# One rounding from VectorE to ScalarE, a score product moved between value products, and an earlier turn of the row of maxima in an attention and soft-MoE kernel

## The chip, the cores and the metric

The kernel runs on one core of one Trainium2 chip. The metric is the device time of one execution in microseconds, lower is better. Engines are named as in the profile: PE is TensorE (PEld its weight loads), DVE is VectorE, ACT is ScalarE, POOL is GpSimd, and SP is the engine that issues the DMAs.

## The reference

Eight batches of eight heads of causal attention with a decay, 576 positions and 64 channels a head, and behind it a soft mixture of eight experts. Cut to what matters here:

```python
scores = scale * np.matmul(q, k.transpose(0, 1, 3, 2))
decay = cum[:, :, :, None] - cum[:, :, None, :]
scores = np.where(causal, -1000000000.0, scores + decay)
scores = scores - np.max(scores, axis=-1, keepdims=True)
attn = np.exp(scores)
attn = attn / (np.sum(attn, axis=-1, keepdims=True) + 1e-09)
attn_out = np.matmul(attn, v)
logits = x @ phi
```

`x` is the attention output as 4608 tokens of 512 channels. The logits then feed a softmax over the tokens (dispatch) and one over the slots (combine), the experts' two products, and the output.

## The kernel before, in words

The 64 heads are taken as 32 pairs. The order of all instructions is written out by hand: each engine runs its own queue in the order in which the code emits it, and waits on semaphores where it needs another engine. An opening does pair 0, parts of pair 1 and the first scores of pair 2; then a loop (line 725 on, `for g in range(1, NG)`) runs one slot for each pair; then a tail does the experts and the output. Scores are computed twice.

First, `s1` (L230, PE) makes scores of queries in rows, with rounded operands, into a PSUM bank named `s`, and `tops` (L244, L246, DVE) takes the maximum of each row of it into a column of `MT`. A head has six such products, numbered 0 to 5. A slot g does the second head of pair g+1 (called u0) and the first head of pair g+2 (u1). When both heads of pair g+1 have their maxima, `mturn` (L256, PE) transposes the columns of `MT` into a PSUM bank, `mrows` copies them out on ACT (L265) and sends them by a DMA from SP (L268, `YA<-mr`) into a row of the operand `YA`. The maxima are thereby subtracted inside the second product.

Second, `s2` (L283 and L284, PE) makes the scores of head h0 and h1 of pair g, keys in rows, into one of three `ring` banks, as a rounded product (L283: `YA`, `WA`) and a correction by the low parts (L284: `YB`, `WB`); `expo` (L290, ACT) takes the exponential of a bank into `PTS`. Segments 0, 1, 2 have a bank each, and segments 3 to 5 share one. `causal` (L298, L301, POOL) blanks the upper triangle. `s3` (L315, PE) multiplies by the values into `pv`, 100 instructions a slot. `norm` (L330 to L335, DVE) divides into `X`. `px` (L342, PE) transposes `X`, and `xcopy` (L372 to L377, ACT) copies it out to `XTS` for the logits.

Operands are prepared ahead: `round_k` (L183) and `round_q` (L188) round on ACT, `dup_q` (L203) and `dup_k` (L199) send the rounded halves by DMA to other partitions, `low_k` and `low_q` (L209, L214, POOL) subtract, and `load_cum` (L194) loads two rows of cumulated decay into `WA`. All DMAs of the loop are issued by SP in one queue.

With `b, w = divmod(g - 4, 4)`, the slots with w = 2 (g = 6, 10, ..., 30) have in addition `combine(b, 0)`, two DVE instructions (L495, L496) ahead of the slot's `tops`, and `dispatch` (L475, PE) ahead of the values. Slots with w = 1 have `mtop` and others.

In the opening the places of the change are the DVE copy of line 625, which rounds the queries of the second head of pair 1; `round_k(1, 1)` (line 630), `expo(0, 3)` (line 631), `dup_q(1, 1, 2)` and `load_cum(2)` behind it; `mturn(1, 0, 1)`, which turns the maxima of head 2; and the stretch from line 654 to 668 with `first(4, 0)`, the first two score products of the first head of pair 2, beside the values of pair 0. `SIDES[0]` is a list of twenty products. `warm(1, cs)` puts PE work without a result into the next `ring` bank.

In the loop they are the two ACT copies of `xcopy(g - 1, (4,))` (L372), `mturn(g + 1)` and `expo(h1, 2)`.

Of the kernel before, what the change touches and what calls it, by code (L numbers as in the profile page):

```python
# [20 lines left out]
NG = B * NPAIR  # L21
# [49 lines left out]
SIDES = [[x for n in zip(units(h, 0, range(4)), units(h, 1, range(4))) for x in n] for h in range(2)]  # L71
# [4 lines left out]
def attn_softmoe(ctx: ExitStack, tc: tile.TileContext, qk, v, f, phi, w1, w2, cst, out):  # L76
    nc = tc.nc
# [102 lines left out]
    def round_k(g, *hs):  # L180
        if pair(g):
            for h in hs or range(2):
                nc.scalar.copy(WA[g % 3][0:64, S * h : S * h + S], RAW[g % 3][64:128, h])  # L183

    def round_q(g, *hs):
        if pair(g):
            for h in hs or range(2):
                nc.scalar.copy(YA[g % 3][0:64, h, 64:640], RAW[g % 3][0:64, h])  # L188
# [45 lines left out]
    def tops(i, *which):  # L234
        if not head(i):
            return
        g, h = divmod(i, 2)
        for n in which:
            bank, o, blk, j0, w = TOPS[n]
            t = st["top", i % 2, bank]  # L240
            m0 = max(448 - (128 * blk + 64) + j0, 0)
            top = MT[g % 3][:, NBLK * h + blk : NBLK * h + blk + 1] if g else m2[h][:, blk, 1:2]
            if n == 2:
                nc.vector.tensor_reduce(top, t[:, o : o + w], axis=AX.X, op=ALU.max)  # L244
                continue
            nc.vector.tensor_tensor_reduce(  # L246
                out=t[:, o : o + w], in0=t[:, o : o + w], in1=mask[:, m0 : m0 + w], scale=1.0, scalar=top.bitcast(F32) if n == 3 else -3.0e38,
                op0=ALU.add, op1=ALU.max, accum_out=top,
            )

    def mturn(g, h0=0, h1=2):

        if not pair(g):
            return
        pm = pv[h0 and 1][:, 384:512]
        nc.tensor.transpose(pm[0 : NBLK * (h1 - h0), 0:128].bitcast(F32R), MT[g % 3][:, NBLK * h0 : NBLK * h1], turner)  # L256
        st["pm", g, h0] = pm
# [29 lines left out]
    def expo(i, bank):  # L287
        if head(i):
            t, at = st["bank"]
            nc.scalar.activation(PT[i % 2][:, SEG_O[bank] : SEG_O[bank] + at], t[:, 0:at], AF.Exp, scale=0.125)  # L290
# [20 lines left out]
    def s3(g, todo):  # L311
        for h, t, u, c in todo:
            r = queries(t, u)
            at = pt_col(c, 64 * r)
            nc.tensor.matmul(  # L315
                pvv[h][64 * u : 64 * u + 64, t, :], PT[h][:, at : at + 64], V[:, g % 2, c, 65 * h : 65 * h + 65], start=(c == 0), stop=(c == r // 2)
            )
# [47 lines left out]
    def xcopy(g, ts):  # L365
        if pair(g):
            n, o = TURN[ts[0]]
            to = XT[g % NPAIR]
            if ts == (4,):
                for h in range(2):  # L370
                    r = slice(64 * h, 64 * h + 64)
                    nc.scalar.copy(to[r, 128:192], pv[n][r, o + 64 * h : o + 64 * h + 64])  # L372
            elif ts == (0, 3):
                to = to[:, 0:384].rearrange("p (n c) -> p n c", c=192)[:, :, 0:128]
                nc.scalar.copy(to, pv[n][:, o : o + 256].rearrange("p (n c) -> p n c", c=128))
            else:
                nc.scalar.copy(to[:, PLACE[ts[0]] : PLACE[ts[0]] + 128 * len(ts)], pv[n][:, o : o + 128 * len(ts)])  # L377
# [221 lines left out]
    def first(i, n, busy=0):  # L599
        s1(i, *GROUPS[n])  # L600
        warm(busy, cs)
        tops(i, *GROUPS[n])

    def both(i, n):
        s2(i, *((0,), (1,), (2,), (3, 4, 5))[n])
        expo(i, n)
# [15 lines left out]
    both(0, 1)  # L622
    first(2, 0)
    both(0, 2)
    nc.vector.tensor_copy(YA[1][0:64, 1, 64:640], RAW[1][0:64, 1])
    next(r1)
    first(2, 1)
    next(r1)
    s2(0, 3, 4, 5)
    round_k(1, 1)  # L630
    expo(0, 3)
    dup_q(1, 1, 2)
    dup_k(1, 1, 2)
# [18 lines left out]
    first(3, 2)  # L652
    first(3, 3)
    round_k(2, 0)
    both(1, 3)
    causal(1)
    low_k(3)
    low_q(3)
    round_q(2, 0)
    s3(0, SIDES[0])  # L660
    mturn(1, 1, 2)
    mrows(1, 1, 2)
    first(4, 0)
    round_k(2, 1)
    round_q(2, 1)
    dup_q(2)
    dup_k(2)
    s3(0, LAST[0])
    norm(0)
    first(4, 1)  # L670
    s3(0, LAST[1] + SIDES[1][:8])
# [53 lines left out]
    for g in range(1, NG):  # L725
        h0, h1 = 2 * g, 2 * g + 1
        u0, u1 = h0 + 3, h0 + 4
        b, w = divmod(g - 4, NPAIR)
        c = b - 1 if w == 0 else b if (b, w) == (B - 2, 3) else None
        if g < 4:  # L730
            load_v(g + 1)
            load_qk(g + 3)
        else:
            load_qk(g + 3)
            load_v(g + 1)
        if 2 <= g < NRES + 2:
            wload(g - 2)
        if w == 1:
            weigh(b)
        low_q(h0 + 2)  # L740
        low_q(h1 + 2)
        s2(h0, 0)
        expo(h0, 0)
        norm(h0 - 1)
        if w == 1:
            mgroup(b)
        if w == 2:
            combine(b, 0)
        s1(u0, 2)
        tops(u0, 2)  # L750
        s2(h0, 1)
        expo(h0, 1)
        s1(u0, 3)
        tops(u0, 3)
        if 1 < g < NG - 1:
            px(g - 1, 0)
        s2(h0, 2)
        expo(h0, 2)
        if g == NG - 1:
            px(g - 1, 0)  # L760
        if g > 1:
            px(g - 1, 3)
        else:
            round_k(3, 0)
            round_q(3, 0)
        s1(u0, 0, 1)
        tops(u0, 0, 1)
        if g > 1:
            px(g - 1, 1)
        s2(h0, 3)  # L770
        if g > 1:
            xcopy(g - 1, (0, 3))
            px(g - 1, 2)
            xcopy(g - 1, (1, 2))
        s2(h0, 4)
        s1(u0, 4, 5)
        s2(h0, 5)
        expo(h0, 3)
        tops(u0, 4, 5)
        causal(h0)  # L780
        low_k(h0 + 2)
        if w == 1:
            mtop(b)
        s2(h1, 0)
        expo(h1, 0)
        if g == 1:
            for t in (0, 3, 1, 2):
                px(0, t)
        px(g - 1, 4)
        if g == 1:  # L790
            xcopy(0, (0, 3))
            xcopy(0, (1, 2))
        xcopy(g - 1, (4,))
        s1(u1, 2)
        tops(u1, 2)
        s2(h1, 1)
        expo(h1, 1)
        s1(u1, 3)
        tops(u1, 3)
        s2(h1, 2)  # L800
        if g < NG - 2:
            expo(h1, 2)
        mturn(g + 1)
        mrows(g + 1)
        if g >= NG - 2:
            expo(h1, 2)
        s1(u1, 0, 1)
        tops(u1, 0, 1)
        s2(h1, 3, 4)
        s1(u1, 4, 5)  # L810
        s2(h1, 5)
        expo(h1, 3)
        tops(u1, 4, 5)
        causal(h1)
        low_k(h1 + 2)
        if g == 1:
            round_k(3, 1)
            round_q(3, 1)
        load_cum(g + 3)
        dup_q(g + 2)  # L820
        dup_k(g + 2)
        if g == 29:
            sides[2].close()
            p2 = fresh(ctx, "p2", 2)
            wstream(*p2, RAW[30 % 3])
        if g == 30:
            sides[1].close()
            xp = ctx.enter_context(tc.tile_pool(name="xp", bufs=1))
            X.append(xp.tile([P, NBLK, 256], F32, name="X3"))
            p0 = fresh(ctx, "p0", 1)  # L830
            p1 = fresh(late, "p1", 3)
            wstream(*p0, *p1, RAW[31 % 3])
        if g == 31:
            sides[0].close()
            with tc.using_default_side("right"):
                tp = ctx.enter_context(tc.tile_pool(name="tp", bufs=1))
            cT = tp.tile([P, sum(CUT)], F32R, name="cT")
            wstream(tp.tile([P, QW], F32, name="w36"))
        if w == 1:
            mcast(b)  # L840
        if c is not None:
            combine(c, 1)
        if w == 2 and b < B - 2:
            dispatch(b, *range(NBLK))
        if g == NG - 1:
            st["lg", B - 1] = scratch(False, f"lg{B - 1}")
            nc.vector.memset(st["lg", B - 1][:, 128:192], -1.0e30)
        round_k(g + 3)
        if w == 1:
            weigh2(b)  # L850
            total(b)
        round_q(g + 3)
        if c is not None:
            combine(c, 2)
        s3(g, VALUES[:30])
        norm(h0)
        if g == 31:
            logits(B - 1, 0, 1)
            wstream(XTS[:, 0:QW], PTS[:, 0:QW])
            split(0, 0)  # L860
            split(1, 0)
        s3(g, VALUES[30:])
        if w == 0:
            logits(b, *range(NPAIR))
        if w == 1:
            tokens(b, 0, 1)
        if g == 28:
            wstream(RAW[29 % 3])
# [272 lines left out]
```

## Time and profile before

| | us |
|---|---|
| runs of the kernel before | 390.41, 391.46, 395.79 |
| their median | 391.46 |
| the profiled execution, its own time | 392.3 |
| its span, first to last instruction | 390.6 |

The span is what the views show; 1.7 us of the profiled execution lie around it. The profiled execution is 0.84 us above the median. Busy shares of the span are PE 95%, PEld 85%, DVE 72%, ACT 69%, POOL 65%. Matmuls overlap and their ends are modelled, so a busy PE can hide a gap shorter than about a matmul's length; the starts of successive instructions tell more.

### The profile page before, as it was taken

To read this page: it belongs to the slowest core of one execution; us is meant where nothing else is said; L and a number is where in the kernel's file an instruction comes from. 1 tells how busy PE (TensorE), PEld (TensorE's weight loads), DVE (VectorE), ACT (ScalarE), POOL (GpSimd) and SP (SyncE) were. 2 spreads that over 40 slices of the span, in tenths; PEclk is the share of its full clock that TensorE was granted. 3 is DMA by queue.
4 is the path that set the end of the run, shared out by engine and by line. 5 is a ranking of instruction groups with operands and counts; after the bars stand their busy time and mean duration, and the time that the engine had idled before them with its cause. 6 is when DMAs were issued, how large, how long until landed. Compare 5 with 4: busy or idle time off the path is not lost.

```text
span 390.6 us, 15123 instructions
## 1 busy us (share of the span) xinstructions
PE 370.5 (95%) x5863; PEld 330.7 (85%) x5863; DVE 281.7 (72%) x1080; ACT 271.3 (69%) x669; POOL 255.0 (65%) x357
## 2 busy tenths in 40 slices
PE   7999999999999999999999999999999998999870
PEld 7789999999999999999999999999999885567640
DVE  7978887878887788788878887878787534341681
ACT  8869887878787778787878787878786553021560
POOL 4897887878787878787878787878787821000000
PEclk9999999999999999999999999999999998999995
DMA  6875978777777777777777777777775899995798
GB/s 205 205 195 148 283 223 278 189 233 207 224 211 215 213 212 214 213 214 211 213 214 214 211 214 212 214 214 212 212 227 154 269 350 377 407 417 206 264 393 314
DMA packets 34344, 93.72 MB, mean 240 GB/s; under 512 B 4266, under 2 KB 8288, under 8 KB 34272
## 3 DMA queue, kind: packets, MB, share of 16 engines
q1 hardware_dynamic: 34272, 92.75, 76.4%
q8 instruction: 46, 0.75, 0.8%
q14 instruction: 26, 0.21, 0.2%
HBM read 63.93 MB, written 9.73 MB: 189 GB/s over the span
## 4 chain that ended last, share of the span: by engine, by line
PE 86%; DMA 6%; POOL 2%; DVE 1%; ACT 1%; issue 1%; POOLq 0%; DVEq 0%; ACTq 0%
PE pv L315 24%; PE ring L283 14%; PE s L230 13%; PE ring L284 13%; PE pv L342 5%; PE pv L981 4%; PE more L941 4%; PE lg L389 3%; DMA out<-RAW 3%; PE ds L475 2%; DMA YA<-mr 2%; DMA WB<-WA 1%; POOL WB L209 1%; DMA PTS<-in_f 1%; POOL YB L214 1%
## 5 line engine op out<-in xcount | busy, mean ns | idle before, releaser
L290 ACT ACTIVATE PTS<-ring 128x320 f32<-128x320 f32 (+2 forms) x256 | 118.1, 502 | 49.3 <-PE ring L284 36.4
L283 PE MATMUL ring<-YA,WA 67*128 67x320 f32 (+9 forms) x384 | 121.5, 330 | 0.8 <-DMA YA<-mr 0.8
L246 DVE CUSTOM_DVE_ANT_0 s<-s,mask 128x320 f32<-128x320 f32 (+3 forms) x256 | 109.0, 442 | 5.6 <-PE s L230 1.1
L284 PE MATMUL ring<-YB,WB 128*128 128x320 f32 (+4 forms) x384 | 110.4, 296 | 0.0
L315 PE MATMUL pv<-V,PTS 128*64 128x65 f32 x3200 | 101.9, 223 | 0.2 <-POOL WB L209 0.2
L315 PEld LDWEIGHTS pv<-V,PTS 128*64 128x64 f32 x3200 | 96.9, 138 | 3.1 <-issue 1.5
L230 PE MATMUL s<-WA,YA 66*128 66x288 f32 (+9 forms) x384 | 98.2, 310 | 0.8 <-DMA RAW<-in_qk 0.4
L209 POOL TENSOR_TENSOR WB<-RAW,WB 64x576 fp32r<-64x576 f32 x64 | 90.4, 1412 | 11.1 <-DMA WB<-WA 5.8
L214 POOL TENSOR_TENSOR YB<-RAW,YA 64x576 fp32r<-64x576 f32 x64 | 89.7, 1421 | 2.6 <-POOL EX L397 0.2
L283 PEld LDWEIGHTS ring<-YA,WA 67*128 67x128 f32 (+3 forms) x384 | 69.7, 183 | 6.3 <-issue 2.1
L284 PEld LDWEIGHTS ring<-YB,WB 128*128 128x128 f32 (+1 forms) x384 | 70.0, 182 | 0.1
L230 PEld LDWEIGHTS s<-WA,YA 66*128 66x128 f32 (+1 forms) x384 | 62.9, 190 | 7.4 <-ACT PTS L290 1.5
L301 POOL TENSOR_SCALAR_AFFINE_SELECT PTS<-PTS 128x128 f32<-128x128 f32 (+1 forms) x128 | 31.5, 268 | 21.1 <-ACT PTS L290 18.6
L246 DVE DVE_READ_ACCUMULATOR2_ANT MT<- 128x1 fp32r x310 | 43.8, 141 | 0.0
L298 POOL TENSOR_SCALAR_AFFINE_SELECT PTS<-PTS 128x384 f32<-128x384 f32 x64 | 33.5, 523 | 14.2 <-ACT PTS L290 10.3
L342 PE MATMUL pv<-cs,X 128*128 128x128 f32 x155 | 42.0, 277 | 0.0
L183 ACT CAST WA<-RAW 64x576 fp32r<-64x576 f32 x64 | 40.1, 668 | 1.0 <-DMA RAW<-in_qk 0.2
L188 ACT CAST YA<-RAW 64x576 fp32r<-64x576 f32 x63 | 39.6, 671 | 0.4
L246 DVE CUSTOM_DVE_ANT_0 s<-s,mask,MT 128x288 f32<-128x288 f32 x62 | 32.6, 526 | 9.3 <-PE s L230 0.4
L330 DVE TENSOR_SCALAR rl<-pv 128x5 f32<-128x5 f32 x64 | 10.5, 164 | 34.0 <-PE pv L315 23.6
L335 DVE TENSOR_TENSOR X<-pv,rl 128x320 f32<-128x320 f32 (+1 forms) x65 | 31.5, 486 | 2.4 <-DMA YA<-mr 0.3
L244 DVE TENSOR_REDUCE MT<-s 128x1 fp32r<-128x288 f32 x62 | 27.8, 449 | 0.4 <-PE s L230 0.4
(221 smaller groups left out, 389.2 us busy)
## 6 DMA issues: line engine op xcount, KB each, us to landing
w<-in_w SPq DMA_DIRECT2D x45, 512.0 KB
RAW<-in_qk SPq DMA_DIRECT2D x31, 576.0 KB
V<-in_v SPq DMA_DIRECT2D x32, 325.0 KB
YB<-YA SPq DMA_DIRECT2D x30, 288.0 KB
WB<-WA SPq DMA_DIRECT2D x30, 288.0 KB
p<-in_w SPq DMA_DIRECT2D x6, 512.0 KB
out<-RAW SPq DMA_DIRECT2D x6, 512.0 KB
out<-p SPq DMA_DIRECT2D x5, 512.0 KB
```

The lines of the kernel that those rows point to most:

```text
L183: nc.scalar.copy(WA[g % 3][0:64, S * h : S * h + S], RAW[g % 3][64:128, h])
L188: nc.scalar.copy(YA[g % 3][0:64, h, 64:640], RAW[g % 3][0:64, h])
L209: nc.gpsimd.tensor_tensor(t[0:64], RAW[g % 3][64:128, h], t[64:128].bitcast(F32), op=ALU.subtract)
L214: nc.gpsimd.tensor_tensor(YB[g % 2][64:128, h], RAW[g % 3][0:64, h], YA[g % 3][0:64, h, 64:640].bitcast(F32), op=ALU.subtract)
L230: nc.tensor.matmul(t[:, o : o + w], ya[0:m, h, 128 * blk : 128 * blk + 128], wa[0:m, j0 : j0 + w], start=True, stop=True)
L246: nc.vector.tensor_tensor_reduce(out=t[:, o : o + w], in0=t[:, o : o + w], in1=mask[:, m0 : m0 + w], scale=1.0, scalar=top.bitcast(F32) if ...
L283: nc.tensor.matmul(o, wa[0:m, j0 : j0 + n], ya[0:m, h, 64 + i0 : 64 + i0 + w], start=True, stop=False)
L284: nc.tensor.matmul(o, wb[:, j0 : j0 + n], yb[:, h, i0 : i0 + w], start=False, stop=True)
L290: nc.scalar.activation(PT[i % 2][:, SEG_O[bank] : SEG_O[bank] + at], t[:, 0:at], AF.Exp, scale=0.125)
L298: nc.gpsimd.affine_select(d3, d3, pattern=[[0, 3], [1, 128]], compare_op=ALU.is_ge, fill=0.0, base=0, channel_multiplier=-1)
L315: nc.tensor.matmul(pvv[h][64 * u : 64 * u + 64, t, :], PT[h][:, at : at + 64], V[:, g % 2, c, 65 * h : 65 * h + 65], start=(c == 0), stop= ...
L342: nc.tensor.transpose(pm[:, 0:128], x[:, t, 128 * (p % 2) : 128 * (p % 2) + 128], ident)
```

## The change

In the opening the rounding of line 625 goes from DVE to ACT, behind `round_k(1, 1)`. `round_q(2, 0)` goes ahead of `both(1, 3)`, and so ahead of its exponential. `first(4, 0)` goes ahead of `mturn(1, 1, 2)`; the list of values is cut at 20, which is the whole of `SIDES[0]`, so the twenty products stay together. In the slots from g = 2 on, `mturn` and `mrows` go ahead of `s2(h1, 2)`, and `xcopy(g - 1, (4,))` goes behind them. `expo(h1, 2)` comes behind them on ACT; before, that was so in the last slots only.

```diff
@@ -622,12 +622,12 @@
     both(0, 1)
     first(2, 0)
     both(0, 2)
-    nc.vector.tensor_copy(YA[1][0:64, 1, 64:640], RAW[1][0:64, 1])
     next(r1)
     first(2, 1)
     next(r1)
     s2(0, 3, 4, 5)
     round_k(1, 1)
+    round_q(1, 1)
     expo(0, 3)
     dup_q(1, 1, 2)
     dup_k(1, 1, 2)
@@ -652,20 +652,20 @@
     first(3, 2)
     first(3, 3)
     round_k(2, 0)
+    round_q(2, 0)
     both(1, 3)
     causal(1)
     low_k(3)
     low_q(3)
-    round_q(2, 0)
-    s3(0, SIDES[0])
+    s3(0, SIDES[0][:20])
+    first(4, 0)
     mturn(1, 1, 2)
     mrows(1, 1, 2)
-    first(4, 0)
     round_k(2, 1)
     round_q(2, 1)
     dup_q(2)
     dup_k(2)
-    s3(0, LAST[0])
+    s3(0, SIDES[0][20:] + LAST[0])
     norm(0)
     first(4, 1)
     s3(0, LAST[1] + SIDES[1][:8])
@@ -790,20 +790,23 @@
         if g == 1:
             xcopy(0, (0, 3))
             xcopy(0, (1, 2))
-        xcopy(g - 1, (4,))
+        if g == 1:
+            xcopy(0, (4,))
         s1(u1, 2)
         tops(u1, 2)
         s2(h1, 1)
         expo(h1, 1)
         s1(u1, 3)
         tops(u1, 3)
+        if g > 1:
+            mturn(g + 1)
+            mrows(g + 1)
+            xcopy(g - 1, (4,))
         s2(h1, 2)
-        if g < NG - 2:
-            expo(h1, 2)
-        mturn(g + 1)
-        mrows(g + 1)
-        if g >= NG - 2:
-            expo(h1, 2)
+        expo(h1, 2)
+        if g == 1:
+            mturn(g + 1)
+            mrows(g + 1)
         s1(u1, 0, 1)
         tops(u1, 0, 1)
         s2(h1, 3, 4)
```

On PE in the opening, in the difference of the two orders, the twenty value products of pair 0 (one row, x20), the first score products of pair 2 (`s_0`) and the turn of the maxima of pair 1 (`MT_110`):

```order
 L284 MATMUL ring_153<-YB_91,WB_92 64x64
 L315 MATMUL pv_149<-V,PTS 64x65 x20
+L230 MATMUL s_0_395<-WA_94,YA_93 128x320
+L230 MATMUL s_0_395<-WA_94,YA_93 128x192
 L256 MATMUL pv_150<-turner,MT_110 5x128
-L230 MATMUL s_0_399<-WA_94,YA_93 128x320
-L230 MATMUL s_0_399<-WA_94,YA_93 128x192
 L315 MATMUL pv_149<-V,PTS 64x65 x5
```

The two score products and the turn have changed places; the values ahead of them are where they were.

On PE in the second half of slot 4 (its other slots from 2 to 30 read alike), the first-pass products of u1 (`s_2`, `s_0`), the turn of the maxima of pair 5 (`MT_111`) and the two instructions of `s2(h1, 2)` (`ring_151`):

```order
 L283 MATMUL ring_153<-YA_85,WA_86 128x320
 L284 MATMUL ring_153<-YB_91,WB_92 128x320
-L230 MATMUL s_2_985<-WA_90,YA_89 128x288
+L230 MATMUL s_2_983<-WA_90,YA_89 128x288
+L256 MATMUL pv_149<-turner,MT_111 10x128
 L283 MATMUL ring_151<-YA_85,WA_86 128x320
 L284 MATMUL ring_151<-YB_91,WB_92 128x320
-L256 MATMUL pv_149<-turner,MT_111 10x128
 L230 MATMUL s_0_995<-WA_90,YA_89 128x320
```

The turn stands two instructions earlier, straight behind the product `s_2`.

On ACT in the second half of slot 5 (a slot like the others), the exponentials of h1 (128x448, then two of 128x320, then 128x512), the copies of `xcopy` and the copy of the row of maxima (`mr`):

```order
 L290 ACTIVATE PTS<-ring_153 128x512
 L290 ACTIVATE PTS<-ring_151 128x448
-L372 COPY XTS<-pv_150 64x64 x2
-L290 ACTIVATE PTS<-ring_152 128x320
-L290 ACTIVATE PTS<-ring_153 128x320
-L265 CAST mr_0_1171<-pv_149 10x128
+L290 ACTIVATE PTS<-ring_152 128x320
+L265 CAST mr_0_1166<-pv_149 10x128
+L372 COPY XTS<-pv_150 64x64 x2
+L290 ACTIVATE PTS<-ring_153 128x320
 L290 ACTIVATE PTS<-ring_151 128x512
```

The copy of the row stood behind two copies and two exponentials; it now stands behind one exponential, and the copies and the second exponential follow it.

## Rows read from the trace of the kernel before

**Rows 1.** The page, part 1: busy time and share of the span, PE.
```profile
PE 370.5 (95%) x5863; PEld 330.7 (85%) x5863; DVE 281.7 (72%) x1080; ACT 271.3 (69%) x669; POOL 255.0 (65%) x357
```

**Rows 2.** Waits of PE from 8 to 310 us: us in total, times, longest.
```profile
PE ring L283 <- DMA YA<-mr: 0.5, 1, 0.5
PE s L230 <- DMA RAW<-in_qk: 0.4, 1, 0.4
PE pv L256 <- POOL WB L209: 0.3, 1, 0.3
PE pv L315 <- POOL WB L209: 0.2, 1, 0.2
```

**Rows 3.** Timeline of the opening, 16.0 to 19.2 us: start, us, engine, line, instruction.
```profile
15.43 1.32 DVE L625 CAST YA<-RAW 64x576 fp32r<-64x576 f32 x1
...
16.09 0.67 ACT L183 CAST WA<-RAW 64x576 fp32r<-64x576 f32 x1
...
16.78 0.47 SPq L203 DMA_DIRECT2D YB<-YA  x1
...
17.57 0.40 PE L230 MATMUL s<-WA,YA 66*128 66x320 f32 x2
...
17.93 0.45 SPq L194 DMA_DIRECT2D WA<-cumd  x1
...
18.13 0.49 PE L511 MATMUL ring<-cs 128*128 128x192 f32 x2
...
18.61 0.14 DVE L246 DVE_READ_ACCUMULATOR2_ANT MT<- 128x1 fp32r x1
...
18.89 0.22 PE L256 MATMUL pv<-turner,MT 128*5 128x128 f32 x1 [0.28 <-POOL WB L209]
```

**Rows 4.** Timeline of the opening, 20.7 to 22.7 us.
```profile
20.75 1.39 PE L315 MATMUL pv<-V,PTS 128*64 128x65 f32 x40
...
22.20 0.50 PE L230 MATMUL s<-WA,YA 66*128 66x320 f32 x2
```

**Rows 5.** Windows of 1 us: length, engines (none here), PEclk, DMA share, GB/s.
```profile
20.00:21.00 1.00, 1.00 0.26 64
```

**Rows 6.** Timeline of slot 4, an ordinary slot, 48.15 to 48.9 us.
```profile
48.20 0.14 DVE L246 DVE_READ_ACCUMULATOR2_ANT MT<- 128x1 fp32r x1
...
48.43 0.31 PE L283 MATMUL ring<-YA,WA 98*128 98x320 f32 x1
...
48.44 0.42 ACT L372 COPY XTS<-pv 64x64 f32<-64x64 f32 x2
48.57 0.31 PE L284 MATMUL ring<-YB,WB 128*128 128x320 f32 x1
...
48.72 0.22 PE L256 MATMUL pv<-turner,MT 128*10 128x128 f32 x1
```

**Rows 7.** Timeline of the same slot, 48.8 to 50.0 us, ACT.
```profile
48.88 0.77 ACT L290 ACTIVATE PTS<-ring 128x320 f32<-128x320 f32 x2
...
49.53 0.24 ACT L265 CAST mr<-pv 10x128 fp32r<-10x128 f32 x1
```

**Rows 8.** Timeline of slot 10, a slot with `combine`, 114.9 to 115.8 us.
```profile
115.08 0.31 PE L283 MATMUL ring<-YA,WA 67*128 67x320 f32 x1
...
115.17 0.14 DVE L246 DVE_READ_ACCUMULATOR2_ANT MT<- 128x1 fp32r x1
...
115.36 0.08 PEld L256 LDWEIGHTS pv<-turner,MT 128*10 128x10 f32 x1
...
115.39 0.30 PEld L230 LDWEIGHTS s<-WA,YA 97*128 97x128 f32 x2
```

**Rows 9.** Line 495, the first instruction of `combine`: ns min/median/max, first and last start.
```profile
L495 DVE TENSOR_REDUCE sm<-tk x7: 326/326/327, 73.2 to 304.2; 128x5 f32<-128x160 f32 x7
```

**Rows 10.** The chain that ended last, 110 to 131 us: start, us, what.
```profile
126.45 3.80 DMA YA<-mr
```

**Rows 11.** Timeline of PE behind slot 30, 303 to 314 us.
```profile
312.28 0.47 PE L283 MATMUL ring<-YA,WA 67*128 67x448 f32 x1 [0.29 <-DMA YA<-mr]
```

## Prediction

> **What bounds the kernel now.** I read the page first: PE is busy for 95% of the span [rows 1]. Then I read the waits of PE for the stretch between the first real products and the end of the attention slots: four waits, 1.4 us together in 302 us [rows 2]. So in the slots PE is the bound, and its instructions start one behind the other. An edit can win there only what is left of those waits, and any new wait of PE is paid in full, because nothing later on PE is waiting that could absorb it. Then I read the timelines at the places of the change, looking at when an instruction starts and when what it needs is done. The tail behind the slots starts when PE gets there, so I let it shift as a block.
>
> **The change part by part: the rounding.** On DVE the cast of line 625 takes 1.32 us; ACT does a cast of the same shape in 0.67 [rows 3]. The last maximum of head 2 is read out at 18.61 for 0.14, so it is there at 18.75, and the turn of PE (L256) starts at 18.89, with 0.28 us of idle before it. The view blames POOL for that wait; its instruction ended at about the same time, but the turn needs `MT`, which DVE writes, so I take DVE as the releaser. Without the cast DVE is earlier by up to 1.32; a third of that is enough to let PE go on at once. The idle of 0.28 is counted from the modelled end of the warm product. In a dense stretch the next product starts 0.16 before such an end: L284 at 48.57 for 0.31 ends at 48.88 and the turn starts at 48.72 [rows 6]. So the gain lies between 0.28 and 0.28 + 0.16 = 0.44; I take 0.4, because the starts are what count.
>
> What the added cast delays: ACT ends `round_k(1, 1)` at 16.09 + 0.67 = 16.76 and the new cast at about 17.44. The product that needs it starts at 17.57 [rows 3], 0.13 later, so PE does not feel it. The exponential behind the cast moves from 16.67 to about 17.46 and ends near 18.05; the warm product that overwrites its bank starts at 18.13, with 0.08 to spare. Were that cover gone, the price would be about 0.1. The DMA of `dup_q(1, 1, 2)`, which waits for this rounding at 16.78 [rows 3], goes out 0.7 later, and with it `dup_k` and `load_cum(2)`, which stand behind it in SP's queue: `load_cum(2)` goes from 17.93 to about 18.64.
>
> **The first maxima of pair 2.** `first(4, 0)` starts at 22.20 now, behind 40 value instructions from 20.75 and the turn [rows 4]. With PE 0.4 earlier and the turn behind it, it could start at 22.20 - 0.4 - 0.14 = 21.66. The total of PE work is unchanged, so the swap is worth nothing by itself. It needs the rows of `load_cum(2)`. The trace shows no landing for them; I bound it. The DMA engines are nearly idle from 20 to 21 (share 0.26) [rows 5], so what was queued before has been moved, and rows issued at 18.64 can be in by about 21; on the other side, the longest time to landing that the chain shows for a short row is 3.80 [rows 10], and 18.64 + 3.80 = 22.44, which would cost 0.78. I take the near end, no wait, since the queue was drained by 21; the far end stays in the range. [...] The rounding `round_q(2, 0)` ahead of the exponential costs ACT nothing new; it is done near 21.0. Opening: -0.4 (bounds -0.44 to +0.4).
>
> **The slots: the turn one score product sooner.** This touches 29 slots. In the new place the turn may start where L283 starts now. In an ordinary slot DVE has the last maximum at 48.20 + 0.14 = 48.34 and PE would be there at 48.43 [rows 6]. How long the signal takes is seen in slot 10: read at 115.17, done at 115.31, the turn's weights start at 115.36, so 0.05 [rows 8]. 48.34 + 0.05 = 48.39, that is 0.04 before PE. So ordinary slots are just free: 0, with a bound of 0.1 if that margin is lost.
>
> In slots with `combine` DVE is later by its two extra instructions of 0.33 each [rows 9]. In slot 10 PE would reach the turn at 115.08, and its maxima let it go at 115.36: even now its weights come straight after the signal. PE is in order there, so it stands still for 115.36 - 115.08 = 0.28, about 0.3 with the matmul's own start, and L283 and L284, which used to fill that time, come behind. The row [rows 9] counts seven such slots. The last is slot 30, where PE already waits 0.29 behind it for the row's DMA at 312.28 [rows 11], so there the loss is absorbed. Six remain: 6 x 0.3 = +1.8. [...]
>
> **The earlier row.** The copy of the row on ACT stood behind two copies (0.42) and two exponentials (0.77) [rows 6, 7]; it now stands behind one exponential, so up to 0.42 + 0.77 / 2 = 0.8 of ACT work is no longer in front of it. The one exponential left there must itself wait for its product on PE, so I take 0.6 for the copy and its DMA, an estimate. That matters where the row lands late: once in 310 us, a landing of 3.80 made PE wait 0.5 [rows 2, 10]. 0.6 covers it: -0.5 (bounds -1.0, when other executions have it twice, to 0, when they don't have it). The copies of `xcopy` and the second exponential come 0.3 to 0.4 later. ACT waits for PE at the next exponential of each slot anyway, the logits that read the copies come at the slot's end or later, and no bank is needed sooner: 0. Without that cover it would be 0.3 a slot.
>
> **Sum.** -0.4 + 1.8 - 0.5 = +0.9. The profiled execution, 392.3 with its 1.7 around the span, would be 393.2. It is 0.84 above the median of the runs, so I put the changed kernel at 391.46 + 0.9 = 392.4.
>
> **Rivals.** *Small gain.* DVE, freed of its lateness by the shift of PE, delivers before PE asks also in the slots with `combine`, and PE keeps only the gains: -0.44 - 0.5 = -0.9, so 390.5. For it: the single waits are real. Against it: DVE's chain in these slots hangs on its own instructions, which don't move.
>
> *Slower, a turn that waits in every slot.* The margin in an ordinary slot is 0.04. If DVE comes only a little later against PE, 23 more slots pay. At 0.1 each it is 1.8 + 2.3 - 0.4 - 0.5 = +3.2, so 394.7; if they become like slot 10, 23 x 0.3 = 6.9 and +7.8, so 399.3. It decides from a lateness of 0.04 on. Against it: DVE is tied to PE by the products it reads, and nothing of its slot work grows.
>
> *Late rows in the opening.* `load_cum(2)` lands at 22.44: +0.78, so the sum is +1.7 and 393.2. For it: SP's queue is one line, and three DMAs move. Against it: the engines drain by 21.
>
> *No effect.* Waits and gains cancel, or the executions don't have the late landing that the profile had: 391.5.
>
> **How the numbers follow.** Forecast (392.4): 0.42. Small gain (390.5): 0.25. Every slot waits: 0.12, of which 0.03 is beyond 2%. Late rows: 0.08. No effect: 0.13. The bounds are -0.44 - 1.0 = -1.4, which is 390.0, and +0.4 + 1.8 + 2.3 = +4.5, which is 396.0; the upper part has little chance, so the range is 389.9 to 395.0. A change of 2% is 7.8 us, about what a measurement of this kernel tells from none. Only the worst case reaches it: slower 0.03, faster 0.01, within 2% 0.96.
>
> **What would show it.** Right: the turn at about 18.45 with no wait before it; no wait at `first(4, 0)`; in slots 6 to 26 with `combine` a PE or PEld wait at L256 for DVE of about 0.3, six in all, and those slots longer by that; the `mr` copy 0.6 earlier. Wrong: L256 without a wait in slot 10, or one in ordinary slots; a wait of L230 for a DMA near 21.7; a span more than 4 us off.

## The result, and the profile after

The changed kernel takes 394.01 us (median of 22 runs, 393.28 to 395.92) beside 390.94 for the kernel before on the same chip (22 runs, 389.62 to 395.97): ratio 1.0090, 95% interval 1.0077 to 1.0102. That is 3.1 to 3.5 us slower, no change by the 2% limit, and inside the range of 389.9 to 395.0. The forecast was +0.9: the direction was right, the size was not. Its 392.4 also stood on a median of three runs, 391.46, half a microsecond above that of the 22. The ratio is taken from the undisturbed executions alone, so it need not be the quotient of the two medians. One label ahead of the prediction is wrong: the rows called slot 4 [rows 6, 7] are of slot 3 (44.30 to 53.07 us), which is as ordinary a slot.

The profiled executions differ by less than the medians: 393.36 (span 391.6) against 392.3 (span 390.6). First the page's line of engines, beside [rows 1]: PE is as busy as before, ACT has gone up.

```profile
PE 371.4 (95%) x5863; PEld 329.9 (84%) x5863; DVE 281.3 (72%) x1079; ACT 275.4 (70%) x670; POOL 254.8 (65%) x357
```

Waits of PE, 8 to 310 us, after, beside [rows 2]: us in total, times, longest. The row `YA<-mr` of 0.5 has gone, and so have the wait of L230 for `RAW` and the wait at the turn (L256); a wait of L230 for ACT's rounding (L188) is new.

```profile
PE s L230 <- ACT YA L188: 0.4, 1, 0.4
PE pv L315 <- POOL WB L209: 0.2, 1, 0.2
```

By this view alone the kernel should have become faster. Where a matmul's modelled end hides a gap, the loads of weights show it. Three rows of the waits of PEld in the same stretch, after; they had no counterpart before but one wait of 0.2 for `MT`:

```profile
PEld pv L256 <- DVE MT L246: 2.3, 6, 0.4
...
PEld pv L342 <- DVE X L335: 1.9, 11, 0.3
...
PEld pv L256 <- DVE row L414: 1.3, 7, 0.2
```

The first is the wait in the six slots with `combine` that was forecast. The second and third were not in the prediction at all. The second stands at the start of a slot, where `px(g - 1, 0)` needs the norm of the previous pair's second head.

Slot 10 after, an answer to [rows 8] (start, us, engine, line). L230 would be followed by the next product some 0.15 later (before, 114.94 to 115.08); the turn stands for the last maximum instead, and L283 comes behind it.

```profile
115.31 0.30 PE L230 MATMUL s<-WA,YA 97*128 97x288 f32 x1
...
115.55 0.14 DVE L246 DVE_READ_ACCUMULATOR2_ANT MT<- 128x1 fp32r x1
...
115.75 0.09 PEld L256 LDWEIGHTS pv<-turner,MT 128*10 128x10 f32 x1 [0.39 <-DVE MT L246]
...
115.81 0.38 PE L283 MATMUL ring<-YA,WA 67*128 67x320 f32 x1
```

Slot 3 after, an answer to [rows 6, 7]: the turn starts 0.13 behind L230 at 47.81, as the next product would, so the margin of 0.04 held. The row's copy is at 48.40; counted from the slot's start (44.30, now 43.74) that is 0.57 earlier than 49.53, the 0.6 of the forecast.

```profile
47.73 0.14 DVE L246 DVE_READ_ACCUMULATOR2_ANT MT<- 128x1 fp32r x1
...
47.81 0.30 PE L230 MATMUL s<-WA,YA 66*128 66x288 f32 x1
47.92 0.09 PEld L256 LDWEIGHTS pv<-turner,MT 128*10 128x10 f32 x1
47.94 0.23 PE L256 MATMUL pv<-turner,MT 128*10 128x128 f32 x1
...
48.40 0.24 ACT L265 CAST mr<-pv 10x128 fp32r<-10x128 f32 x1
```

The start of slot 16, before and then after (the brackets hold idle time and releaser). Counted from the slot's first L283, the second head's norm (L330) starts at 0.11 and then at 0.19, and L342 follows at 1.09 and then 1.16. DVE's idle time in front of L330 is 0.20 and then 0.27.

```profile
168.72 0.47 PE L283 MATMUL ring<-YA,WA 67*128 67x448 f32 x1
168.83 0.16 DVE L330 TENSOR_SCALAR rl<-pv 128x5 f32<-128x5 f32 x1 [0.20 <-PE pv L315]
...
169.81 0.32 PE L342 MATMUL pv<-cs,X 128*128 128x128 f32 x1
```

```profile
169.52 0.47 PE L283 MATMUL ring<-YA,WA 67*128 67x448 f32 x1
169.71 0.17 DVE L330 TENSOR_SCALAR rl<-pv 128x5 f32<-128x5 f32 x1 [0.27 <-PE pv L315]
...
170.68 0.14 PEld L342 LDWEIGHTS pv<-cs,X 128*128 128x128 f32 x1 [0.15 <-DVE X L335]
170.68 0.33 PE L342 MATMUL pv<-cs,X 128*128 128x128 f32 x1
```

The compiled order says why. Such a norm of one pair, before and after (`PE_49` and `Activation_49` are the semaphores that PE and ACT raise):

```
L330 TENSOR_SCALAR rl_775<-pv_150 128x5 [waits PE_49]
L330 TENSOR_SCALAR rl_775<-pv_150 128x5 [waits PE_49,Activation_49]
```

It reads the bank that `xcopy(g - 1, (4,))` reads on ACT. Before, that copy stood ahead of the row's copy on ACT, and the first head's norm, which waits for the row's copy anyway, covered it. Now the copy stands behind the row, and the second head's norm needs a wait of its own, 23 times in the kernel. In the packed trace it appears as an extra semaphore instruction on DVE ahead of the norm: in slot 16 after, one that waits for PE stands at 169.64, 0.07 ahead of L330, and L330 itself then waits for ACT; before, L330 waits for PE there and has none. Of these extra instructions at L330 there are 26 before and 49 after. Of the 23 new ones 14 are in slots with w = 0 or w = 3. Seven more are in slots with w = 2, where they cost nothing: there the norm began 0.24 to 0.32 ahead of the slot's first L283 and now begins 0.11 to 0.17 ahead, and L342 stays at 1.06 to 1.09.

In the slots with w = 1, `mtop`'s reduction of the row of maxima stands on DVE behind the last maximum and reads the turn's bank. Slot 9 after:

```profile
105.58 0.27 DVE L414 TENSOR_REDUCE row<-pv 1x32 f32<-1x128 f32 x1
...
105.91 0.09 PEld L256 LDWEIGHTS pv<-turner,MT 128*10 128x10 f32 x1 [0.18 <-DVE row L414]
```

The opening after, beside [rows 3]: the rounding ends at 17.51 and L230 waits 0.40 for it; the turn starts at 18.43, where the forecast had it, but on a way that it did not have.

```profile
16.16 0.67 ACT L183 CAST WA<-RAW 64x576 fp32r<-64x576 f32 x1
16.84 0.67 ACT L188 CAST YA<-RAW 64x576 fp32r<-64x576 f32 x1
...
17.57 0.50 PE L230 MATMUL s<-WA,YA 66*128 66x320 f32 x2 [0.40 <-ACT YA L188]
...
18.43 0.36 PE L256 MATMUL pv<-turner,MT 128*5 128x128 f32 x1
```

The wait of 0.28 at the turn is gone, and so is one of 0.37 ahead of it, which [rows 2] puts down to `RAW` and the weight load's row to POOL, which clears a part of `YA` in line 578. That wait is not the cast's: e12 has the changed opening and 0.18 of it, and in both profiles POOL's subtraction (L214) began latest of all, at 15.01 and 15.15. Before, then e12, where the line is 580:

```profile
16.94 0.19 PEld L230 LDWEIGHTS s<-WA,YA 66*128 66x128 f32 x1 [0.67 <-POOL YA L578]
16.94 0.30 PE L230 MATMUL s<-WA,YA 66*128 66x64 f32 x1 [0.37 <-DMA RAW<-in_qk]
```

```profile
16.88 0.30 PE L230 MATMUL s<-WA,YA 66*128 66x64 f32 x1 [0.18 <-POOL YA L580]
```

Where the time went, by slots. A slot's length is the distance between the first L283 (67x448) of two successive slots on PE's timeline; the table has the differences to the kernel before's profile, summed, in us. The last row is the sum over slots 1 to 30, slots 1 and 2 included.

| slots | after | e2 | e3 | e4 | e5 | e6 | e11 | e12 |
|---|---|---|---|---|---|---|---|---|
| six with `combine` | 2.15 | 2.08 | 0.38 | 0.05 | 1.74 | 1.75 | 2.17 | 1.31 |
| w = 0 and w = 3, without 11 | 1.30 | 0.21 | 1.26 | 1.18 | 1.26 | 0.14 | 0.41 | 1.23 |
| w = 1 | 0.24 | 0.22 | 0.23 | -0.10 | 0.24 | 0.22 | 0.26 | 0.21 |
| slot 11 | -0.50 | -0.58 | -0.50 | -0.52 | -0.48 | -0.57 | -0.58 | -0.48 |
| slot 30 | -0.24 | -0.28 | -0.01 | -0.19 | -0.38 | -0.37 | -0.24 | -0.36 |
| sum | 2.97 | 1.66 | 1.34 | 0.47 | 2.91 | 1.33 | 2.21 | 1.92 |

With slot 1 starting 0.60 earlier (25.70 for 26.30) and a tail shorter by 1.3 (below), the span comes out 1.1 longer.

One profile is one execution. The five others whose turn and copies stand where they stood (e1 and e7 to e10) come out at -0.21 to 0.18 in the first row, -0.05 to 0.30 in the second, -0.19 to 0.15 in the third, -0.60 to 0.03 in slot 11 and -0.37 to 0.09 in slot 30, so that much is no effect of these edits. The +0.24 with w = 1 is small beside that, but all seven profiles with the early turn in those slots have 0.21 to 0.26. The wait at L414 itself was not tried apart.

### The profile page after: what moved, and what is told of

It is laid out like the page before. It is cut to its first block, busy times and chain, and to the rows that moved or that the text cites. A ratio compares the mean times of both kernels' runs of the same rounds, so it can differ in the third digit from the quotient of the medians.

```text
span 391.6 us, 15145 instructions
## 1 busy us (share of the span) xinstructions
PE 371.4 (95%) x5863; PEld 329.9 (84%) x5863; DVE 281.3 (72%) x1079; ACT 275.4 (70%) x670; POOL 254.8 (65%) x357
## 4 chain that ended last, share of the span: by engine, by line
PE 76%; DVE 8%; ACT 7%; DMA 5%; issue 1%; SPq 1%; POOL 0%; ACTq 0%; DVEq 0%; POOLq 0%
PE pv L315 20%; PE ring L283 12%; PE ring L284 11%; PE s L230 10%; PE pv L342 4%; PE pv L984 4%; DVE s L246 4%; PE more L944 4%; PE lg L389 3%; PE ring L511 2%; DMA out<-RAW 2%; PE ds L475 2%; ACT WA L183 2%; ACT YA L188 2%; DMA WB<-WA 1%
## 5 line engine op out<-in xcount | busy, mean ns | idle before, releaser
L290 ACT ACTIVATE PTS<-ring 128x320 f32<-128x320 f32 (+2 forms) x256 | 119.6, 502 | 45.9 <-PE ring L284 35.2
L283 PE MATMUL ring<-YA,WA 67*128 67x320 f32 (+9 forms) x384 | 123.2, 334 | 0.0
L284 PE MATMUL ring<-YB,WB 128*128 128x320 f32 (+4 forms) x384 | 110.4, 296 | 0.0
L230 PE MATMUL s<-WA,YA 66*128 66x288 f32 (+9 forms) x384 | 96.2, 306 | 1.0 <-ACT YA L188 0.4
L214 POOL TENSOR_TENSOR YB<-RAW,YA 64x576 fp32r<-64x576 f32 x64 | 89.7, 1420 | 2.6 <-POOL EX L397 0.2
L283 PEld LDWEIGHTS ring<-YA,WA 67*128 67x128 f32 (+3 forms) x384 | 69.7, 183 | 5.2 <-issue 2.1
L284 PEld LDWEIGHTS ring<-YB,WB 128*128 128x128 f32 (+1 forms) x384 | 69.9, 182 | 0.0
L230 PEld LDWEIGHTS s<-WA,YA 66*128 66x128 f32 (+1 forms) x384 | 64.0, 190 | 5.9 <-ACT PTS L290 1.9
L342 PE MATMUL pv<-cs,X 128*128 128x128 f32 x155 | 42.1, 278 | 0.1
L188 ACT CAST YA<-RAW 64x576 fp32r<-64x576 f32 x64 | 40.2, 670 | 0.4
L330 DVE TENSOR_SCALAR rl<-pv 128x5 f32<-128x5 f32 x64 | 10.5, 164 | 36.6 <-PE pv L315 27.0
```

The source lines that it names most:

```text
L214: nc.gpsimd.tensor_tensor(YB[g % 2][64:128, h], RAW[g % 3][0:64, h], YA[g % 3][0:64, h, 64:640].bitcast(F32), op=ALU.subtract)
L230: nc.tensor.matmul(t[:, o : o + w], ya[0:m, h, 128 * blk : 128 * blk + 128], wa[0:m, j0 : j0 + w], start=True, stop=True)
L283: nc.tensor.matmul(o, wa[0:m, j0 : j0 + n], ya[0:m, h, 64 + i0 : 64 + i0 + w], start=True, stop=False)
L284: nc.tensor.matmul(o, wb[:, j0 : j0 + n], yb[:, h, i0 : i0 + w], start=False, stop=True)
L342: nc.tensor.transpose(pm[:, 0:128], x[:, t, 128 * (p % 2) : 128 * (p % 2) + 128], ident)
```

## The experiments

Two losses were to be told apart, the turn's wait in the slots with `combine` and the second wait of the norm, and the opening to be weighed by itself. Each ratio is to the kernel before on the same chip, with its 95% interval.

**e1, the opening alone.** The four edits above the loop, and the loop of the kernel before.

> The opening's edits alone, the slots as in the kernel before. The traces of the two kernels put the start of slot 1 at 26.30 before and 26.02 after. Theory: the opening is worth -0.28 and nothing of it is given back in the slots, so 390.9 - 0.3 = 390.6, ratio 0.999. Rival 1 (my prediction's term of -0.4): 390.5. Rival 2: the gain is given back at the first place where PE waits for something that keeps its time (the RAW landing in slot 3): 390.9, and slot 4 would start where it did before.

Measured: 390.28 against 390.38, ratio 0.9999 (0.9988 to 1.0010). The 26.02 in the expectation is misread: the timeline of after has slot 1 at 25.70, e1 at 25.63. So the view promised 0.6 to 0.7, and the time shows nothing; its interval reaches from -0.5 to +0.4 us, so that a gain of 0.4 is not excluded. Part of the reason came with e4.

**e2, the copies back in their old place.**

```diff
-        if g == 1:
-            xcopy(0, (4,))
+        xcopy(g - 1, (4,))
         s1(u1, 2)
...
             mrows(g + 1)
-            xcopy(g - 1, (4,))
```

> The changed kernel with the two copies xcopy(g-1, (4,)) back in their old place, ahead of the row of maxima; the turn stays in its new place. Theory (second wait): behind the row's copy, these copies make the norm of a pair's second head wait for ACT besides PE, which costs about 0.07 a slot in some 22 ordinary slots and 0.25 in slot 8; with the copies in their old place that wait is covered by the wait of the first head's norm for the row's copy, so 394.0 - 1.6 = 392.4, and the waits of PEld at L342 for X (1.9 us, 11 times) go. Rival (the copies cost nothing, as my prediction had it; the turn's new place makes all of the loss): 394.0, within 0.3.

Measured: 393.15, ratio 1.0085 (1.0055 to 1.0114), above the 392.4 of the theory. Of its six runs three had a mean granted clock of 0.984 and took 394.0 to 396.2; the three at 0.988 took 392.2 to 392.3, 2.0 more than the kernel before at 0.987 or more (17 runs, median 390.24). The trace is clearer: the group L342 for `X` is gone, L342 is back at 1.09, there are 26 extra semaphore instructions at L330 again, and the slots lose 1.66 instead of 2.97. So the second wait is worth 1.3, not 1.6.

**e3, the old turn in the slots with `combine`.**

```diff
+        early = g > 1 and w != 2
-        if g > 1:
+        if early:
             mturn(g + 1)
             mrows(g + 1)
             xcopy(g - 1, (4,))
         s2(h1, 2)
         expo(h1, 2)
-        if g == 1:
+        if not early:
             mturn(g + 1)
             mrows(g + 1)
+            if g > 1:
+                xcopy(g - 1, (4,))
```

> The changed kernel, but in the slots with combine (w = 2) the turn, the row and the copies xcopy behind it come where the turn stood before, behind the exponential. Theory: the turn's wait for the last maximum in six such slots is 0.36 to 0.41 each, 2.2 together; without it 394.0 - 2.2 = 391.8, and the waits of PEld at L256 for MT (2.3 us, 6 times) go. Rival: DVE is late in these slots anyway, and PE waits for it a little later (at the next product that needs a bank from DVE): less than half of it comes back, 393.0 or more.

Measured: 391.54, ratio 1.0036 (1.0017 to 1.0055), 0.0054 below the changed kernel's, 2.1 us. The first theory holds: of 2.15 in those six slots 0.38 is left. The waits for `X` stay, and there are three more of them:

```profile
PEld pv L342 <- DVE X L335: 2.4, 14, 0.4
```

**e4, the copies behind the row, nothing else.**

```diff
-        xcopy(g - 1, (4,))
+        if g == 1:
+            xcopy(0, (4,))
         s1(u1, 2)
...
         mturn(g + 1)
         mrows(g + 1)
+        if g > 1:
+            xcopy(g - 1, (4,))
```

> The kernel before with one edit: the two copies xcopy(g-1, (4,)) come behind the row's copy on ACT, and the turn stays in its old place. Theory (second wait): DVE's second norm gets its wait for ACT, 0.07 in some 25 slots = +1.6, so 390.9 + 1.6 = 392.5. Rival (the copies' place costs nothing): 390.9, within 0.3. A third reading: the copies ahead of the slot's last exponential hold it up by 0.42, which would cost up to 0.3 a slot, 9 us and 400; then a wait of PE for a ring bank or for PTS would show.

Measured: 391.81, ratio 1.0034 (1.0018 to 1.0049), +1.3. Of the third reading's 0.3 in each slot nothing is seen. The turn is where it was before, the 49 extra semaphore instructions at L330 are there, and so are the waits at L342:

```profile
PEld pv L342 <- DVE X L335: 2.4, 13, 0.5
```

This run has the old opening, and it explains most of e1. Counted from PE's first L230, it reaches slot 1 after 17.54 us; the kernel before needed 18.31 in its profile, the changed one 17.53. The cast of line 625 took 0.57, not 1.32 [rows 3]. Cast and POOL's subtraction, in the profile of before, of e8 (same opening) and of e4:

```profile
15.43 1.32 DVE L625 CAST YA<-RAW 64x576 fp32r<-64x576 f32 x1
15.01 1.42 POOL L214 TENSOR_TENSOR YB<-RAW,YA 64x576 fp32r<-64x576 f32 x1
```

```profile
15.39 1.08 DVE L625 CAST YA<-RAW 64x576 fp32r<-64x576 f32 x1
14.74 1.41 POOL L214 TENSOR_TENSOR YB<-RAW,YA 64x576 fp32r<-64x576 f32 x1
```

```profile
15.41 0.57 DVE L625 CAST YA<-RAW 64x576 fp32r<-64x576 f32 x1
13.86 1.42 POOL L214 TENSOR_TENSOR YB<-RAW,YA 64x576 fp32r<-64x576 f32 x1
```

In the first two the cast ends 0.32 behind the end of the subtraction (16.75 behind 16.43, 16.47 behind 16.15). In the third the subtraction was over at 15.28. POOL's place differs by over a microsecond between executions (13.86 to 15.01 here). So the cast took 1.32 and 1.08 where the subtraction still ran beside it, and 0.57 where it was over (0.45 in e7, where it was over at 14.74). That POOL holds the cast up is my inference from these four; by what means, no run shows. Of the three profiles of the old opening two have the overlap; they reach slot 1 after 18.31, 18.04 (e8) and 17.54, the eight of the whole changed opening after 17.53 to 17.75.

**e5 and e6, `combine` at the slot's end; and with it the copies as in e2.**

```diff
-        if w == 2:
-            combine(b, 0)
         s1(u0, 2)
...
         tops(u1, 4, 5)
+        if w == 2:
+            combine(b, 0)
```

> The changed kernel with the two DVE instructions of combine(b, 0) moved from the slot's first maxima to its end, behind the last maxima; the turn and the copies xcopy stay as changed. Theory: the turn waits in these slots because DVE carries 0.65 us more ahead of the last maximum; without them in front, the six waits of PEld at L256 for MT go, and the slots with w = 2 lose their 0.36 each: about -2.0 against the changed kernel, so a ratio of about 1.004 to the kernel before, as in the run with the old turn in those slots. Rival: DVE is the bound of these slots, wherever the two stand; then the wait comes back at the next slot's first score product or at its values, and the ratio stays at 1.007 or more.

> The run before this one, and the copies xcopy(g-1, (4,)) back ahead of the row as well. Theory: the two losses are independent and add, 2.0 and 1.3; what is left of the changed kernel's slots is the late row that is gone (-0.5 in slot 11, -0.2 in slot 30) and the turn's wait behind mtop in the slots with w = 1 (+0.2): the slots end 0.3 to 0.6 earlier than in the kernel before, ratio 0.998 to 1.001. Rival: one of the two losses covers the other, so that taking both away gives little more than the larger: ratio 1.003 or more.

Measured: e5 393.37, ratio 1.0079 (1.0055 to 1.0102); e6 392.19, ratio 1.0047 (1.0034 to 1.0060). The six waits at L256 went, but the rival's ratio came out; e6 missed as well. The wait had moved, in e5:

```profile
PE ds L475 <- DVE MT L246: 1.6, 6, 0.3
```

`dispatch` (L475) and, by the weight loads, a first-pass product (L230) wait for DVE now. The bank `tk`, which `combine` reads, is of the same pool as theirs, and is held until `combine` has run; that this is the cause is inferred and was not tried apart. So these two don't show what the turn costs; e3 and e12 do. What e6 has over e5, the copies in their old place, is 0.0032, 1.25 us: the second wait again.

**e7, the swap of `first(4, 0)` and the turn alone** (rounding on DVE, `round_q(2, 0)` early).

> Of the opening's edits, the order of first(4, 0), of the turn and of round_q(2, 0) alone; the rounding of line 625 stays on DVE, the slots as before. Counted from PE's first L230: the opening of the kernel before reaches slot 1 after 18.31 us in its profile (cast of 1.32 us) and after 17.54 in the run with the copies behind the row (same opening, cast of 0.57 us); the changed opening after 17.53 to 17.65. Theory: the swap is worth nothing, so 17.5 if the cast takes about 0.6, 18.3 if it takes 1.3, and no wait of PE for ACT at L230; time as before, ratio 1.000 within 0.001. Rival: the swap is what costs the 0.1, and the wait of 0.4 for the rounding is made good behind it: 17.65 with a short cast.

Measured: 390.71, ratio 1.0004 (0.9988 to 1.0021). The cast took 0.45, and slot 1 came after 17.70: the rival. `first(4, 0)` now stands before its rows are in, though `load_cum(2)` was issued at 17.28:

```profile
21.56 0.47 PE L230 MATMUL s<-WA,YA 66*128 66x320 f32 x2 [0.27 <-DMA WA<-cumd]
```

So the late rows of my third rival exist. The semaphore that these rows raise comes to its last step at 21.42 here, 4.1 behind the issue. In the changed kernel, which issues them at 18.70, it does so at 20.84, 2.1 behind, and L230 at 21.55 does not wait. Over the fourteen profiles it takes 2.1 to 4.1, and longest where the rows are issued early (3.6 to 4.1 for issues up to 17.93); why stays open.

**e8, e9, e10: what might be kept.** e8 is the kernel before with `expo(h1, 2)` behind the turn and the row in every slot; e9 the kernel before with the rounding on ACT; e10 both.

> The kernel before with one edit in the slots: the exponential expo(h1, 2) comes behind the turn and the row in all slots, as it did in the last ones; the turn keeps its old place on PE, the copies xcopy theirs. The row's copy on ACT then stands behind one exponential fewer, some 0.4 earlier. Theory: most of the late landing in slot 11 (0.5) goes and nothing else changes, as neither the turn waits for DVE nor the norm for ACT: -0.3 to -0.5, so a ratio of 0.999. Rival: the row's copy on ACT now waits for the turn on PE and holds up the exponential behind it, which would show as waits of PE for a ring bank in many slots: ratio 1.002 or more.

> Of the opening's edits, the rounding on ScalarE alone (line 625 goes from DVE to ACT behind round_k(1, 1)); everything else as before. Theory: PE waits 0.4 at L230 for the rounding, as in the changed kernel; in exchange DVE is never held by a cast that took 1.32 us in one profile and 0.57 in another, so the opening takes 17.5 to 17.6 us from PE's first L230 to slot 1 whatever the execution, against 17.54 to 18.31 in three profiles of the old opening. In the time: ratio 0.998 to 1.000. Rival: the wait of 0.4 is added to the old opening at its best, 17.9, and the ratio is 1.001.

> The rounding on ScalarE, and in all slots the exponential expo(h1, 2) behind the turn and the row; the turn, the copies xcopy and first(4, 0) in their old places. Theory: what the change holds of use, without its two losses: -0.6 in slot 11 and -0.2 to -0.4 in slot 30 from the earlier row, and 0 to -0.3 in the opening: -0.5 to -1.0, so 389.3 to 389.9 beside 390.3, ratio 0.9975 to 0.999. Rival: the gains sit in places where the next wait takes them back, ratio 1.000.

Measured: e8 390.06, ratio 0.9991 (0.9977 to 1.0006); e9 390.64, ratio 1.0004 (0.9990 to 1.0017); e10 390.04, ratio 0.9998 (0.9982 to 1.0015). None can be told from the kernel before; e10's forecast of 0.9975 to 0.999 is not borne out, nor excluded. In e9 PE waits 0.4 at L230, as expected, and reaches slot 1 after 17.71, between the 17.6 of the theory and the 17.9 of the rival, in e10 after 17.59: the old opening at its best (17.54) and 0.05 to 0.17 more. Slot 11 is 0.6 shorter in e8 and e10, but also in e9, whose row is where it was. So the late landing [rows 2, 10] is not in every execution: three of four profiles with the row in its old place have it (before, e1, e7), none of ten with an earlier row. Slot 30 is 0.24 to 0.37 shorter in e7, e8, e9 and e10 too, whose slot 30 is as it was.

**e11, the late copies on the other bank.** The transpose that the copies read goes to `pv[0]`, columns 256 to 384, but in slots with w = 1. This overwrites constants in the unused half of the last block of rows, so that half of `X` is not the reference's; the work is the same.

```diff
+    def place(g, t):
+        return (0, 256) if t == 4 and g > 0 and (g + 1 - 4) % 4 != 1 else TURN[t]
```

> The changed kernel, its copies xcopy(g-1, (4,)) as late as changed; but the transpose px(g-1, 4), which they read, goes into a free part of the other pv bank (not in the slots with w = 1, where mtop uses that part). Then the norm of the first head, which waits for ACT anyway because of the row in that bank, waits for the copies too, and the norm of the second head waits for PE alone, in three slots of four. Theory (it is the second wait of that norm that costs, not that the copies are late): about three quarters of what the run with the early copies gave back, 0.9 us: ratio 1.006 to 1.0075, and the waits of PEld at L342 for X go but for the slots behind w = 1. Rival (the copies are late, and hold ACT and the exponential behind them): nothing comes back, ratio 1.009, waits at L342 as before.

Measured: 393.26, ratio 1.0086 (1.0054 to 1.0117), which separates nothing. The trace does: the copies are as late as changed, yet L342 is at 1.09 again and its waits are gone but for one.

```profile
PEld pv L342 <- DVE X L335: 0.2, 1, 0.2
```

Of the extra semaphore instructions at L330 33 are left, the seven beyond 26 in slots with w = 2. So it is the second wait of that norm, not the lateness of the copies, that costs.

**e12, the turn one product later in the slots with `combine`**, between L283 and L284 of `s2(h1, 2)`.

> The changed kernel, but in the slots with combine the turn stands between the two products of s2(h1, 2), one product (0.15 to 0.2 us) later than changed and one earlier than before. Theory: what the turn costs in these slots is the time that PE stands at it, so each gives back what PE now does in that time, 0.15 to 0.2 of 0.36 to 0.41, six times: -1.0, ratio 1.006 to 1.007. Rival: PE is in such a slot held by DVE as a whole (the first-pass banks), and a turn that waits only moves the waiting: less than 0.3 comes back in all.

Measured: 393.24, ratio 1.0068 (1.0049 to 1.0087): theory. The six slots lose 1.31 instead of 2.15; slot 10 (beside 0.39 above):

```profile
115.62 0.09 PEld L256 LDWEIGHTS pv<-turner,MT 128*10 128x10 f32 x1 [0.23 <-DVE MT L246]
```

## Why the size was wrong

**Six slots with `combine`, +1.8: right, 2.15.** The mechanism is the one foretold: place, releaser and number of waits [rows 8, 9]. Each costs 0.29 to 0.41, not 0.3. Slot 30 absorbed it: its turn waits longer still, 0.62, and the slot is no longer than before.

**"The copies of `xcopy` ... come 0.3 to 0.4 later ...: 0": the step that failed most, +1.3.** I asked who needs the data of the copies, and no one does sooner. I did not ask who waits for their reading of the bank. Moving them behind the row took away the cover of a wait that had been free (e2, e4, e6, e11). It falls in 14 slots (w = 0 and w = 3), about 0.07 at L342 each and 0.27 in slot 8; why slot 8 pays more was not looked into.

**Ordinary slots 0: right for the turn itself** [rows 6], but not with w = 1, where `mtop` is queued behind the last maximum: +0.24.

**Opening -0.4: wrong in its working, 0 in the time** (e1, which leaves -0.5 to +0.4). The step that failed is the cast at 1.32 [rows 3]. It was read from an execution in which POOL's subtraction ran beside the cast, as in e8 (1.08) and not in e4 and e7 (0.57, 0.45), and the added rounding "0.13 later, so PE does not feel it" leaned on a product that this same execution had made late, behind its wait of 0.37. In nine of the ten profiles with the rounding on ACT, L230 comes first and waits 0.4. The near end that the forecast took for the rows of `load_cum(2)`, in "by about 21", was right (20.84, beside the 22.44 of the far end), though not as a rule: in the kernel before, whose packed trace does show the landing, they were in at 21.50, 3.6 behind the issue.

**Earlier row -0.5: seen in slot 11, not shown.** The changed kernel's profile has the gain, and no profile with an earlier row has the late landing; but e9, with the row in its old place, hasn't either, and e8 and e10, with the earlier row, are not told from the kernel before in time. The 0.24 in slot 30 can't be put down to the row: in e7 to e10, whose slot 30 is as it was, it is as short.

**Sum.** 0 + 2.15 + 1.30 + 0.24 - 0.50 - 0.24 = +2.95, beside a measured +3.1 to +3.5. The two negative terms are one profile against another, so the agreement is partly luck. The rival "a turn that waits in every slot" named 394.7, near the result, by the wrong mechanism: its turns in ordinary slots don't wait.

The forecast was put on the median, but the profile it was read from was an unlucky one: the cast, the late row and a fall of the clock (next section) all fell into it, so that two gains were counted that other executions have less of.

## What to carry over

When an instruction is moved past another on its engine, list who waits for either, and which wait had covered the other; the order with its waits shows a second semaphore before any time does. A duration two or three times that of its like may go with another engine's work beside it, as here (1.32 and 1.08 beside POOL's subtraction, 0.57 and 0.45 without): ask whether it comes in each execution before counting it as a gain. And in a kernel bound by PE, read the waits of the weight loads too: the matmuls' own showed none of the 2.3, 1.9 and 1.3 us of waiting that came in. Such a wait shows where to look and not what it costs: in slot lengths the three were worth 2.15, 1.30 and 0.24.

## What was not expected of the hardware

The tail behind the slots, from slot 31's first L283 to the end, takes 78.3 to 78.6 us in five of the fourteen profiles and 76.9 to 77.3 in the other nine. The five have a mean granted clock of 0.984 to 0.986, the others 0.987 to 0.990, and the kernel before's profile is one of the five. Its window from 328 to 329 us (PEclk is the third number from the end) has a granted clock of 0.50; the line ahead of it is of 326 to 332 (0.72), and the fence behind it has that window after, at 1.00 throughout.

```profile
326.00:332.00 6.00, 4.92 (x66) 3.48 (x69) 2.53 (x10) 1.66 (x9) 0.79 (x3) 0.72 1.00 376
...
328.00:329.00 1.00, 1.00 (x28) 0.92 (x24) 0.00 (x0) 0.11 (x1) 0.00 (x0) 0.50 1.00 369
```

```profile
326.00:332.00 6.00, 4.90 (x79) 3.04 (x72) 3.35 (x12) 1.99 (x9) 1.13 (x4) 1.00 0.98 360
```

The fall to 0.50 begins at 327.09, at the end of an idle PE of 0.8 us, and lasts 3.41 us, but the changed kernel's profile has the same idle time at the same product and no fall there. Before, then after:

```profile
327.03 0.67 PE L711 MATMUL more<-cs,cw 128*128 128x128 f32 x2 [0.81 <-DVE cw L696]
```

```profile
329.52 0.44 PE L711 MATMUL more<-cs,cw 128*128 128x128 f32 x2 [0.82 <-DVE cw L696]
```

So an execution with the fall may be about 1.4 us longer than one without, as much as the second wait. The times say much the same: of the 75 executions of the kernel before that were run beside the experiments, the 16 with a mean granted clock of 0.984 to 0.986 have a median of 391.1, the other 59 of 390.2. Why it falls in some executions stays open, and so does what shifts POOL in the opening.
